# The bias stage of an attention and two-layer kernel: where two splits run, and on which engine four masks are made

## The chip, the cores and the metric

The kernel runs on one core of a Trainium2 chip. The metric is the device time of one execution in microseconds (us). The core has five engines with a queue each: TensorE (PE, matmuls into PSUM), VectorE (DVE), ScalarE (ACT), GpSimd (POOL) and SyncE (SP), which here only issues DMAs. PEld is PE's weight load, which is shown apart.

## The reference

Three steps follow one another; all is fp32.

- Attention over 4 batches, 8 heads, 576 positions, head size 64: `scores = q @ k.T / 8 + bias`, a softmax, and the product with `v`. The bias is the same for every batch. It comes from a small network of the relative position: `x[i,j] = log1p(|i-j|) / log1p(max(i,1))`, `h = relu(x * w1 + b1)` with 32 hidden units, `bias = h @ w2`, one value for each head.
- A dense layer with a leaky activation: 2304 tokens, 512 to 2048 and back to 512.
- A soft routing: 32 slots get a softmax-weighted mean of the tokens, each of 8 experts runs two layers on its 4 slots, and each token gets a softmax-weighted mean of the slots' results.

## The kernel before

The program runs through the bias stage (about the first 75 us), attention for 16 pairs (a pair of heads and a batch each, about 13 us a pair), the dense layer with the routing beside it, and the experts. It is written in a framework that plans the order of each engine's queue offline, by simulated times and by the order in which the instructions stand in the program. `keep_in_program_order(ins)` (a pin) ties an instruction behind the instruction of the same engine that stands before it in the program; without a pin the plan may move it.

**Bias stage** (`bias_phase`, lines 70 to 285). A relu of a linear function of x is a linear function where x is above a threshold and zero elsewhere. So the stage makes masks (is log1p(|i-j|) above the threshold of this hidden unit?), and matmuls sum them, weighted, into two accumulators a0 and a1; the bias is `a0 * x + a1`. The work goes in nine rounds k = 0 to 8 over relative distance. A round has 16 masks of 576 columns or, from round 5 on, 512, 384, 256 and 128 (`make_mask`, line 135), in a ring of 40 (`RING`): mask u of round k reuses the place of the mask that was made 40 earlier. Table `ENGS` says by a letter which engine makes each mask: A is ACT with a steep sigmoid (line 142), V is DVE with a comparison (line 144). A round has up to five units c = 3, 2, 1, 0 and, in rounds 0 to 4, 4 (`unit`, line 148). A unit is 48 matmuls (16 masks by 3 parts of the weights, line 160) into one of four accumulators, then its evacuation on DVE: a product (line 189) and a sum into `rows` (line 193, or 191 for c = 4). Then POOL writes the mirrored half of `rows` (line 211; called a flip here). When a chunk of rounds is complete, SP stores the rows into W in DRAM (line 216). The masks of round k + 1 are written between the units of round k (lines 264 to 275).

`att.load(0)` and `att.load_v(0)` load pair 0 before the rounds, `att.load(1)` and `att.load_v(1)` stand behind them. `att.bias_first(s)` (line 347) loads the bias of the first pair of heads back from W, piece s, at the end of rounds 5 and 7 and behind the rounds. The stores for the other heads (`late`) come last.

**Attention** (`Attention`, line 288). Each of q and k of a pair is split into a high half, rounded to the matmul format, and a low half, the rest (`split`, line 371): k = 0 makes `qh` (1216 columns), 1 `ql`, 2 `kh` (576 columns), 3 `kl`, all on POOL (lines 380 and 382). For pair 0 the four stand at the ends of rounds 0 to 3 of the bias stage:

```python
if k < 4:
    att.split(0, k)
```

For pair 1 they stand at the head of `run` (line 545), and none of the eight is pinned. In the trace POOL runs both pairs' splits between 14 and 30 us. Later pairs are split two pairs ahead. `raw`, the loaded pair, has two buffers. Scores are matmuls of line 412, 60 for a pair; then DVE adds the bias and takes the minimum (`z`, line 435), ACT takes the exponential (line 455), PE transposes (line 475), ACT or DVE copies (lines 491 and 489), and PE multiplies with v (line 503). Attention's order is written out by hand in `ROUND`, and from pair 1 on all of it is pinned.

Of the kernel before, what the change touches and what calls it, by code (L numbers as in the profile page):

```python
# [8 lines left out]
F32 = mybir.dt.float32  # L9
# [4 lines left out]
AF = mybir.ActivationFunctionType  # L14
ALU = mybir.AluOpType
# [26 lines left out]
TAGS = ("cfgc", "becb", "gbd", "ada", "mnm")  # L42
LATE, EARLY = "bcdg", "aefmn"
ENGS = (
    "VVVAVVAVVAVVAVVA", "AAAVAAAVAAAVAAAV", "AAAVAAAVAAAVAAAV", "AAAVAAAVAAAVAAAV", "AAAVAAAVAAAVAAAV", "AAVAAVAAVAAVAAVA",
    "AAVAAVAAVAAVAAVA", "AVAAVAVAAVAVAAVA", "AVAVAVAAVAVAVAVA",
)
LA = 5
# [18 lines left out]
BIG = float(2.0 ** 20)  # L67


def bias_phase(tc, ident, W, W4, cpack, lcol, prow, xmain, xtail, att):  # L70


    nc = tc.nc
    with ExitStack() as ctx:
# [13 lines left out]
        pr = cp.tile([P, S], F16, name="pr")  # L88
# [10 lines left out]
        wb = cp.tile([P, NTQ], F32, name="wb")  # L99
# [27 lines left out]
        for k in range(3):  # L127
            eng = nc.gpsimd if k < 2 else nc.vector
# [6 lines left out]
        def make_mask(k, u):  # L135

            t = 16 * k + u
            n = min(S, 128 * (NG - k))
            dst = mask[:, t % RING, :n]
            on = ENGS[k][u]  # L140
            if on == "A":
                nc.scalar.activation(dst, pr[:, :n], AF.Sigmoid, bias=wb[:, t : t + 1], scale=BIG)  # L142
            else:
                nc.vector.tensor_scalar(dst, pr[:, :n], wl[:, t : t + 1], None, ALU.is_gt)

# [2 lines left out]
        def unit(k, c):  # L148
# [4 lines left out]
            if c < 4:  # L153
                m, cols, dst = P, slice(P * c, P * c + P), acc
            else:
                m, cols = 64 * (k % 2) + 64, slice(512, S)
                dst = acc[m - 64 : m]
# [12 lines left out]
            i = max(n for n in range(len(ks)) if ks[n] <= k)  # L170
# [14 lines left out]
            fwd = both[:m, :, :, w + f0 : w + f0 + 64]  # L185
            tmp = cp.tile([P, H, 2, 32], F32, tag="tmp", name=f"tmp{k}_{c}", bufs=2)
            xb = xs.rearrange("p (s j) -> p s j", s=2).unsqueeze(1).to_broadcast([m, H, 2, 32])
            a0, a1 = (acc[:m, :, n].rearrange("p s h j -> p h s j") for n in range(2))
            nc.vector.tensor_tensor(tmp[:m], a0, xb, ALU.mult)
            if c == 4:  # L190
                nc.vector.tensor_tensor(fwd[:, :, 0].rearrange("p h (s j) -> p h s j", s=2), tmp[:m], a1, ALU.add)
            else:
                nc.vector.tensor_tensor(  # L193
                    fwd.rearrange("p a b (s j) -> p a b s j", s=2),
                    tmp[:m].rearrange("p (a b) s j -> p a b s j", b=2),
                    a1.rearrange("p (a b) s j -> p a b s j", b=2),
                    ALU.add,
                )

            one = d0 == 0 and c < 4  # L200
            z = int(one and f0 == 0)
            a = both[:m, :, :, w + one - f0 - 64 : w + one - f0 - z]
            if c == 4:
                a, src = a[:, :, 0], fwd[:, :, 0]
            else:
                src = fwd[:, :, :, z:]
            e = a.ap[-1][0]
            back = bass.AP(
                tensor=a.tensor, offset=a.offset + (63 - z) * e, ap=[list(v) for v in a.ap[:-1]] + [[-e, 64 - z]]
            )  # L210
            nc.gpsimd.tensor_scalar(back, src, 1.0, 1.0, ALU.mult, ALU.mult)
            if not last:
                return

# [42 lines left out]
        for u in range(16):  # L257
            make_mask(0, u)
# [5 lines left out]
        for k in range(NG):  # L264
            cs = [c for c in range(3, -1, -1) if k <= NG - 1 - c]
            if k < 5:
                cs.append(4)
            done = 0
            for n_, c in enumerate(cs):
                unit(k, c)  # L270
                if k + 1 < NG:
                    upto = 16 * (n_ + 1) // len(cs)
                    for u in range(done, upto):
                        make_mask(k + 1, u)
                    done = upto
            if k < 4:
                att.split(0, k)
            if k in (5, 7):
                att.bias_first(k // 7)
        att.load(1)  # L280
# [7 lines left out]
class Attention:  # L288
# [82 lines left out]
    def split(self, i, k):  # L371

        st = self.st[i]
        x = "qk"[k // 2]
        src = st["raw"][:, :1216] if x == "q" else st["raw"][:, 1216:]
        if k % 2 == 0:
            st[x, 0], st[x, 1] = (
                self.sp.tile([P, src.shape[1]], F32R, tag=x + "hl"[n], name=f"{x}{'hl'[n]}{i}") for n in range(2)
            )
            self.nc.gpsimd.tensor_scalar(st[x, 0], src, 1.0, 1.0, ALU.mult, ALU.mult)  # L380
        else:
            self.nc.gpsimd.tensor_tensor(st[x, 1], src, st[x, 0].bitcast(F32), ALU.subtract)  # L382

    def late(self, i, ins):

# [865 lines left out]
def kernel(  # L1251
# [17 lines left out]
        for n, b in (("a_raw", 2), ("a_v", 3), ("a_split", 2))  # L1269
    )  # L1270
    bias_phase(tc, ident, W, W4, cpack, lcol, prow, xmain, xtail, att)

    kp = ctx.enter_context(tc.tile_pool(name="m_keep", bufs=1, reuse_waits="tile"))
# [178 lines left out]
```

## Time and profile before

| | us |
|---|---|
| median of 3 runs | 804.72 (804.67 to 805.17) |
| the profiled execution | 801.72 |
| its span, first to last instruction | 799.9 |

| engine | busy us | share of the span | instructions |
|---|---|---|---|
| PE | 760.0 | 95% | 7438 |
| DVE | 531.0 | 66% | 999 |
| ACT | 503.5 | 63% | 1053 |
| POOL | 323.8 | 40% | 283 |

A row of instructions has the start in us, the time in us, engine, line, operation, output<-inputs, shapes and count; in brackets the idle time of the engine before it and what ended that. "issue" means that the engine waited for nothing that the profile shows. Times of single instructions overlap a little from one to the next.

### The profile page before, as it was taken

To read this page: it belongs to the slowest core of one execution; us is meant where nothing else is said; L and a number is where in the kernel's file an instruction comes from. 1 tells how busy PE (TensorE), PEld (TensorE's weight loads), DVE (VectorE), ACT (ScalarE), POOL (GpSimd) and SP (SyncE) were. 2 spreads that over 40 slices of the span, in tenths; PEclk is the share of its full clock that TensorE was granted. 3 is DMA by queue.
4 is the path that set the end of the run, shared out by engine and by line. 5 is a ranking of instruction groups with operands and counts; after the bars stand their busy time and mean duration, and the time that the engine had idled before them with its cause. 6 is when DMAs were issued, how large, how long until landed. Compare 5 with 4: busy or idle time off the path is not lost.

```text
span 799.9 us, 18597 instructions
## 1 busy us (share of the span) xinstructions
PE 760.0 (95%) x7438; PEld 636.4 (80%) x7438; DVE 531.0 (66%) x999; ACT 503.5 (63%) x1053; POOL 323.8 (40%) x283
## 2 busy tenths in 40 slices
PE   6877899999999999999999999999999999999994
PEld 6876777777787778999898888888889898887431
DVE  8878788888898856776777566546654746544203
ACT  8973788888888854444456666656665656654102
POOL 4723253646465713114225554445553551240000
PEclk9999799999999999999999999999999999999898
DMA  6597975738444641433420011301100124349895
GB/s 202 141 251 198 307 242 199 237 95 297 145 123 152 186 159 63 141 119 105 147 90 1 1 40 41 131 1 41 40 1 21 40 78 159 107 134 358 318 376 237
DMA packets 48406, 114.44 MB, mean 143 GB/s; under 512 B 10433, under 2 KB 29761, under 8 KB 46273
## 3 DMA queue, kind: packets, MB, share of 16 engines
q1 hardware_dynamic: 48320, 113.26, 43.0%
q8 instruction: 58, 0.95, 0.5%
q14 instruction: 28, 0.22, 0.1%
HBM read 91.95 MB, written 21.29 MB: 142 GB/s over the span
## 4 chain that ended last, share of the span: by engine, by line
PE 80%; DVE 4%; DMA 4%; ACT 1%; issue 1%; POOL 1%; SPq 0%; DVEq 0%; ACTq 0%
PE ys L757 25%; PE h L728 24%; PE o L503 9%; PE s L412 8%; PE t L475 4%; PE ops L1211 3%; PE hps L1211 2%; DVE z L435 1%; DMA W<-rows 1%; PE acc L160 1%; PE lp L826 1%; DMA raw<-in_qk_dram 1%; DMA em<-in_mw_dram 1%; DMA nb<-W 1%; DMA rs<-rt 1%
## 5 line engine op out<-in xcount | busy, mean ns | idle before, releaser
L739 DVE SCALAR_TENSOR_TENSOR g<-g,nal 128x384 f32<-128x384 f32 x96 | 70.2, 731 | 93.8 <-ACT g L738 93.8
L435 DVE CUSTOM_DVE_ANT_0 z<-s,nb 128x576 f32<-128x576 f32 x144 | 108.0, 754 | 18.0 <-PE s L412 9.4
L455 ACT ACTIVATE e<-z,m 128x576 f32<-128x576 f32 x144 | 109.9, 767 | 7.6 <-DVE m L435 7.6
L736 ACT ACTIVATE g<-h 128x384 f32<-128x384 f32 x96 | 47.1, 490 | 64.8 <-PE h L728 63.5
L491 ACT ACTIVATE g<-t 128x640 f32<-128x640 f32 x96 | 67.3, 703 | 30.7 <-PE t L475 26.6
L503 PE MATMUL o<-g,v 128*64 128x256 f32 (+1 forms) x640 | 85.3, 411 | 0.5 <-ACT g L491 0.5
L744 DVE TENSOR_TENSOR gr<-g,gr 128x384 fp32r<-128x384 f32 x80 | 63.7, 797 | 29.2 <-ACT gr L742 29.1
L475 PE MATMUL t<-ident,e 64*128 64x64 f32 x1440 | 69.1, 225 | 5.4 <-DVE m L435 4.3
L475 PEld LDWEIGHTS t<-ident,e 64*128 64x128 f32 x1440 | 66.5, 141 | 7.4 <-issue 5.5
L160 PE MATMUL acc<-wp,mask 128*128 128x64 bf16 (+1 forms) x1680 | 57.2, 199 | 15.7 <-issue 6.6
L742 ACT ACTIVATE gr<-g 128x384 fp32r<-128x384 f32 x96 | 50.3, 524 | 34.3 <-DVE g L739 34.1
L160 PEld LDWEIGHTS <-mask 128*128 128x128 bf16 (+1 forms) x1680 | 55.5, 104 | 17.3 <-DVE rows L193 6.4
L503 PEld LDWEIGHTS o<-g,v 128*64 128x64 f32 x640 | 43.3, 136 | 28.4 <-ACT g L491 1.0
L412 PE MATMUL s<-kh,qh 64*128 64x288 f32 x320 | 62.1, 384 | 1.3 <-DVE rows L193 0.7
L142 ACT ACTIVATE mask<-pr,wb 128x576 bf16<-128x576 f16 (+4 forms) x94 | 54.8, 675 | 8.1 <-PE acc L160 8.0
L412 PE MATMUL s<-kh,ql 64*128 64x288 f32 x320 | 48.5, 298 | 0.0
L412 PE MATMUL s<-kl,qh 64*128 64x288 f32 x320 | 48.5, 298 | 0.0
L744 POOL TENSOR_TENSOR gr<-g,gr 128x384 fp32r<-128x384 f32 x16 | 19.2, 1200 | 71.9 <-ACT gr L742 51.9
L738 ACT ACTIVATE g<-h 128x384 f32<-128x384 f32 x96 | 46.7, 487 | 0.0
L380 POOL TENSOR_SCALAR qh<-raw 128x1216 fp32r<-128x1216 f32 x16 | 19.5, 1218 | 66.7 <-PE s L412 61.3
L382 POOL TENSOR_TENSOR ql<-raw,qh 128x1216 fp32r<-128x1216 f32 x16 | 44.9, 2807 | 0.0
L412 PEld LDWEIGHTS s<-kh,qh 64*128 64x128 f32 x320 | 31.5, 192 | 10.5 <-DVE r L522 4.2
(851 smaller groups left out, 1838.8 us busy)
## 6 DMA issues: line engine op xcount, KB each, us to landing
wide<-in_w_dram SPq DMA_DIRECT2D x16, 1024.0 KB
ep<-in_mw_dram SPq DMA_DIRECT2D x29, 512.0 KB
raw<-in_qk_dram SPq DMA_DIRECT2D x16, 896.0 KB
nb<-W SPq DMA_DIRECT2D x3, 2304.0 KB
v<-in_v_l_dram SPq DMA_DIRECT2D x16, 320.0 KB
pre<-in_mw_dram SPq DMA_DIRECT2D x10, 512.0 KB
ex<-in_mw_dram SPq DMA_DIRECT2D x9, 512.0 KB
W<-rows SPq DMA_DIRECT2D x14, 256.0 KB
```

Of the source, the lines that this page charges most:

```text
L142: nc.scalar.activation(dst, pr[:, :n], AF.Sigmoid, bias=wb[:, t : t + 1], scale=BIG)
L160: nc.tensor.matmul(dst[:, u // 8, :, :, 4 * (u % 8) : 4 * (u % 8) + 4], mask[:, (16 * k + u) % RING, cols], wp[:, part], start=part == 0, ...
L412: nc.tensor.matmul(s[:, hf, :288], st["q", a][d, o : o + P], st["k", b][d, 288 * h : 288 * h + 288], start=n_ == 0, stop=n_ == len(seq) - 1,),
L435: self.nc.vector.tensor_tensor_reduce(out=z.rearrange("p (a b) -> p a b", a=2), in0=s[:, :, :288], in1=nb.rearrange("p (a b) -> p a b", a= ...
L455: self.nc.scalar.activation(e, z, AF.Exp, bias=m, scale=-1.0, accum_out=st["sum"][:, slot : slot + 1]),
L475: self.pin(i, nc.tensor.transpose(tp[:, r, 64 * c : 64 * c + 64], e[q, k0 : k0 + P], self.ident[q, q]))
L491: self.pin(i, nc.scalar.activation(dst, src, AF.Copy))
L503: nc.tensor.matmul(op[64 * h : 64 * h + 64, 0, :n], st["v"][:, h, c], g[:, h, c], start=c == 0, stop=c == 4),
L728: nc.tensor.matmul(h, w_[:, c * P : (c + 1) * P], x_[:, c], start=c == 0 and n_ == 0, stop=c == NC - 1 and n_ == 2,)
L739: nc.vector.scalar_tensor_tensor(g, neg, self.nal[:, f : f + 1], g, ALU.mult, ALU.add)
L744: eng.tensor_tensor(gl, g, gh.bitcast(F32), ALU.subtract)
L757: i = self.nc.tensor.matmul(self.ys[blk][t], g_[:, t * P : (t + 1) * P], w_, start=f == 0 and n_ == 0, stop=f == NF - 1 and n_ == 2,)
```

## The change

In the bias stage:

- `ENGS`: rounds 1 to 4 have 11 masks on ACT and 5 on DVE, where they had 12 and 4.
- Pair 0's split leaves the ends of rounds 0 to 3. Its high halves `qh` and `kh` are copies on ACT, behind round 5's masks (end of round 4); its low halves `ql` and `kl` are subtractions on DVE, at the end of round 5. All four are pinned.
- Pair 1's split stays on POOL and is pinned, so that it stands behind all flips.
- Masks on ACT, the sums into `rows` on DVE and the flips on POOL are pinned.

```diff
-    "VVVAVVAVVAVVAVVA", "AAAVAAAVAAAVAAAV", "AAAVAAAVAAAVAAAV", "AAAVAAAVAAAVAAAV", "AAAVAAAVAAAVAAAV", "AAVAAVAAVAAVAAVA",
+    "VVVAVVAVVAVVAVVA", "AAVAAVAAVAAVAAVA", "AAVAAVAAVAAVAAVA", "AAVAAVAAVAAVAAVA", "AAVAAVAAVAAVAAVA", "AAVAAVAAVAAVAAVA",
...
-                nc.scalar.activation(dst, pr[:, :n], AF.Sigmoid, bias=wb[:, t : t + 1], scale=BIG)
+                i = nc.scalar.activation(dst, pr[:, :n], AF.Sigmoid, bias=wb[:, t : t + 1], scale=BIG)
+                tc.keep_in_program_order(i)
...
+            tc.keep_in_program_order(i_)
...
-            nc.gpsimd.tensor_scalar(back, src, 1.0, 1.0, ALU.mult, ALU.mult)
+            tc.keep_in_program_order(nc.gpsimd.tensor_scalar(back, src, 1.0, 1.0, ALU.mult, ALU.mult))
...
-            if k < 4:
-                att.split(0, k)
+            if k in (4, 5):
+                att.split(0, k - 4)
+                att.split(0, k - 2)
...
-            self.nc.gpsimd.tensor_scalar(st[x, 0], src, 1.0, 1.0, ALU.mult, ALU.mult)
+            if i == 0:
+                self.early(1, self.nc.scalar.activation(st[x, 0], src, AF.Copy))
+                return
+            self.early(i, self.nc.gpsimd.tensor_scalar(st[x, 0], src, 1.0, 1.0, ALU.mult, ALU.mult))
         else:
-            self.nc.gpsimd.tensor_tensor(st[x, 1], src, st[x, 0].bitcast(F32), ALU.subtract)
+            eng = self.nc.gpsimd if i else self.nc.vector
+            self.early(max(i, 1), eng.tensor_tensor(st[x, 1], src, st[x, 0].bitcast(F32), ALU.subtract))
+
+    def early(self, i, ins):
+
+        if i == 1:
+            self.tc.keep_in_program_order(ins)
```

## Rows read from the trace of the kernel before

**Rows 1.** The page, part 1: busy us, share of the span, instructions.

```profile
PE 760.0 (95%) x7438; PEld 636.4 (80%) x7438; DVE 531.0 (66%) x999; ACT 503.5 (63%) x1053; POOL 323.8 (40%) x283
```

**Rows 2.** Windows: length, each engine's busy us, granted clock, DMA share, GB/s.

```profile
13.80:31.00 17.20, 13.18 (x376) 12.82 (x374) 17.09 (x20) 17.20 (x27) 16.58 (x15) 0.90 0.29 109
51.90:74.90 23.00, 19.66 (x620) 19.12 (x616) 22.94 (x47) 9.59 (x24) 9.26 (x14) 1.00 0.79 180
80.00:90.00 10.00, 8.21 (x88) 7.27 (x88) 7.25 (x19) 6.93 (x16) 0.00 (x0) 0.57 1.01 281
100.00:110.00 10.00, 10.00 (x147) 7.68 (x144) 8.33 (x21) 8.13 (x19) 7.50 (x6) 1.00 1.02 364
```

**Rows 3.** Waits of PE, 0 to 75 us: total us, times, longest us.

```profile
PE acc L160 <- issue: 6.6, 5, 2.6
...
PE acc L160 <- DVE rows L193: 3.5, 2, 2.2
```

**Rows 4.** Timeline of PE around 30 us.

```profile
30.52 9.81 PE L160 MATMUL acc<-wp,mask 128*128 128x64 bf16 x298 [2.20 <-DVE rows L193]
```

**Rows 5.** Timeline of DVE in the bias stage.

```profile
16.84 4.35 DVE L144 TENSOR_SCALAR mask<-pr,wl 128x576 bf16<-128x576 f16 x2
...
30.99 0.42 DVE L144 TENSOR_SCALAR mask<-pr,wl 128x576 bf16<-128x576 f16 x1
...
36.14 0.36 DVE L144 TENSOR_SCALAR mask<-pr,wl 128x576 bf16<-128x576 f16 x1
...
51.93 1.29 DVE L189 TENSOR_TENSOR tmp<-acc,xm_t 128x512 f32<-128x512 f32 x2 [3.69 <-PE acc L160]
```

**Rows 6.** Groups of DVE, 13.8 to 31 us: count, busy us, mean ns, idle before.

```profile
L144 DVE TENSOR_SCALAR mask<-pr,wl 128x576 bf16<-128x576 f16 x8 | 10.9, 1401 | 0.0
```

**Rows 7.** Timeline of POOL in the bias stage.

```profile
16.80 2.78 POOL L382 TENSOR_TENSOR ql<-raw,qh 128x1216 fp32r<-128x1216 f32 x1
...
74.92 0.68 POOL L211 TENSOR_SCALAR rows<-rows 128x512 f32<-128x512 f32 x1 [0.62 <-DVE rows L193]
```

**Rows 8.** Timeline of ACT in the bias stage.

```profile
5.23 45.19 ACT L142 ACTIVATE mask<-pr,wb 128x576 bf16<-128x576 f16 x70
52.92 4.64 ACT L142 ACTIVATE mask<-pr,wb 128x384 bf16<-128x384 f16 x10 [2.50 <-PE acc L160]
61.62 3.57 ACT L142 ACTIVATE mask<-pr,wb 128x256 bf16<-128x256 f16 x10 [4.07 <-PE acc L160]
```

**Rows 9.** Windows of line 160 alone: PE, PEld, clock, DMA share, GB/s.

```profile
25.69:35.49 9.80, 7.59 (x243) 7.30 (x240) 1.00 0.54 155
35.49:44.29 8.80, 7.97 (x243) 7.57 (x241) 1.00 1.07 308
44.29:51.69 7.40, 4.79 (x123) 4.70 (x120) 0.77 1.09 326
```

**Rows 10.** Window of pair 2's split: POOL is the fifth busy time.

```profile
95.40:101.60 6.20, 6.20 (x102) 4.98 (x96) 5.19 (x12) 5.50 (x12) 6.01 (x4) 1.00 0.99 409
```

**Rows 11.** Window of line 412 alone, up to pair 1's first scores.

```profile
73.60:87.76 14.16, 7.19 (x60) 5.63 (x62) 0.77 0.84 251
```

**Rows 12.** Groups over the whole span: busy us, mean ns, idle before.

```profile
L491 ACT ACTIVATE g<-t 128x640 f32<-128x640 f32 x96 | 67.3, 703 | 30.7 <-PE t L475 26.6
...
L682 DVE SCALAR_TENSOR_TENSOR wr<-wide,wr 128x1024 uint32<-128x1024 uint32 x14 | 17.1, 1222 | 0.3
...
L716 DVE TENSOR_TENSOR w47o<-wr,w47o 128x512 fp32r<-128x512 f32 x1 | 0.7, 693 | 0.9 <-ACT w47o L715 0.9
```

**Rows 13.** The chain of waits at the end of the stage: start us, us, what.

```profile
70.60 0.67 POOL rows L211
...
71.59 4.42 DMA W<-rows
...
77.04 3.72 DMA W<-rows
...
80.83 4.98 DMA nb<-W
```

More of the change, by code (lines that the diff above doesn't have):

```diff
@@ L190, in unit @@
             if c == 4:
-                nc.vector.tensor_tensor(fwd[:, :, 0].rearrange("p h (s j) -> p h s j", s=2), tmp[:m], a1, ALU.add)
+                i_ = nc.vector.tensor_tensor(fwd[:, :, 0].rearrange("p h (s j) -> p h s j", s=2), tmp[:m], a1, ALU.add)
             else:
-                nc.vector.tensor_tensor(
+                i_ = nc.vector.tensor_tensor(
                     fwd.rearrange("p a b (s j) -> p a b s j", s=2),
```

## The prediction

> **What bounds the kernel now.** I read the page first: TensorE (PE) is busy 95% of the span of 799.9 us [rows 1]. An average over stages says little about a change in the first 75 us, so the table of windows came next. From 13.8 to 31 us PE is busy 13.18 of 17.20 us and VectorE (DVE) 17.09; from 51.9 to 74.9 PE 19.66 of 23.00 and DVE 22.94 [rows 2]. So PE has room in the bias stage, and DVE is full at its beginning and at its end. From 100 us on PE is busy 10.00 of 10.00 us [rows 2]: attention is paced by PE, so what the stage gains or loses arrives at the end of the kernel one for one. The question is only how much earlier the stage hands over.
>
> The waits of the stage [rows 3]: PE stopped five times, 6.6 us in all, up to "issue": it waited for no semaphore that the profile shows, and none of the edits names a cause of that. It stopped twice, 3.5 us, for DVE's `rows`: an accumulator was not free, because DVE was late in emptying it. The larger of the two, 2.20 us, ends at 30.52 [rows 4].
>
> DVE's rows say why it was late then. From 13.8 to 31 us it made eight masks in 10.9 us, 1401 ns each [rows 6]; an undisturbed mask of that shape is the one at 36.14 us, 0.36 us [rows 5]. Beside them GpSimd (POOL) ran the splits of pairs 0 and 1: the two masks that start on DVE at 16.84 take 4.35 us [rows 5], while `ql` on POOL runs from 16.80 for 2.78 us [rows 7] and `kl` after it. So the eight masks took 10.9 - 8 x 0.36 = 8.0 us of DVE more than they take alone.
>
> ScalarE (ACT) makes 70 masks without a gap from 5.23 us on, 45.19 us, so 0.645 us each, and then waits for PE, 2.50 us and later 4.07 [rows 8]. At 50.4 us it is ahead of PE, not behind: on the chip its masks no longer hold PE in rounds 3 and 4. That matters for the third edit below.
>
> **Part by part.** All sums are made against the profiled execution (span 799.9, execution 801.72 us). The median of the three timed runs, 804.72, lies 3.0 us above it; the difference found is applied to that.
>
> *Pair 0's split leaves POOL's early rounds, pair 1's goes behind the stage.* DVE's 8.0 us go. Only what PE waited for can reach the end, and that is its one stop on DVE there: -2.2 us [rows 4]. The rest of the 8.0 becomes idle time of DVE, since rounds 1 to 3 are then fed as fast as PE runs. Late next is PE itself: round 2 keeps it busy 7.59 us in a window of 9.80 [rows 9].
>
> *Pair 1's split, now behind the last flip.* That flip starts at 74.92 and takes 0.68 us [rows 7]. A pair's four split operations take POOL 6.01 us [rows 10], so they are done at 81.6. PE needs them for the first scores of pair 1; pair 0's 60 matmuls of line 412 fill the window up to 87.76, and pair 1 follows [rows 11]. The cover is 6 us, and both ends move with the stage: cost 0. Nothing else is queued on POOL before pair 2's split, and no DMA is added; the load of pair 3, which needs the buffer that this split frees, is issued a round of attention later. On the gaining side, the flips of rounds 0 to 3 no longer queue behind a `ql` of 2.8 us, so SyncE's first W stores may leave up to that much earlier, into a stretch in which the DMA engines are 0.29 busy [rows 2]; I take 0 for it.
>
> *Pair 0's high halves on ACT, behind the masks of round 5.* Scaled by columns from the 640-column copy of 703 ns [rows 12]: 0.703 x (1216 + 576)/640 = 2.0 us. Scaled by the masks' 0.645 us for 576 columns it would also be 2.0. Behind them wait round 6's masks. ACT idles 2.50 us in that round and 4.07 in the next, for PE [rows 8], so cost 0; without that cover, round 6 would start up to 2.0 us late.
>
> *One mask of each of rounds 1 to 4 from ACT to DVE.* ACT -4 x 0.645 = -2.6 us; DVE +4 x 0.36 = +1.4, or 4 x (0.36 + 0.68) = 4.2 if each waits for a flip on POOL. Another mask beside POOL's work, at 30.99, took 0.42 [rows 5], so nearer the first. DVE has them where it has just lost 8.0 us of delay: cost 0. On ACT the gain is worth nothing directly, since ACT is ahead of PE. It can matter for the written order: in round 4, from 44.29 on, PE loads 120 masks before DVE starts the next evacuation at 51.93 [rows 5, 9], where one unit is 48, because PE's order interleaves a round's units around masks that were planned to come late. With ACT's masks planned earlier there is less to interleave. Ends: 0, and all of the 72 matmuls beyond one unit, 72 x 7.59/243 = 2.2 us [rows 9]. No row says which; I take -1.3, a little over the middle, because by round 4 the plan too has been relieved of 2.6 us of ACT.
>
> *Pair 0's low halves on DVE in round 5.* Operations with two inputs from SBUF: 693 ns at 512 columns, 1222 at 1024 [rows 12], so 1.03 ns a column: 1.42 us for 1216 columns and 0.76 for 576, together 2.2. They stand behind a mask of round 6 whose place in the ring comes free in round 4's last unit, so they fall in the stretch from 51.9, where DVE is busy 22.94 of 23.00 us [rows 2]. Behind them wait the evacuations of rounds 5 to 7, and for those POOL's flips and the last W stores. Ends: 0, if they find gaps or stand behind the last evacuation, and 2.2. The nearest row is that of a full DVE, so most of it counts; but where round 4's first evacuation comes earlier, gaps open between units, since PE takes 1.5 us for a unit (48 x 7.59/243) and DVE 1.3 (two operations of 0.65, [rows 5]): +1.5.
>
> On this edit the page "SBUF — State Buffer" of the Trainium skill, section "Summary: rules for kernel authors", speaks against the change: an operation of VectorE with two SBUF inputs fully blocks against a GpSimd operation that reads SBUF, as one in a 2-port fast mode does. The flips read SBUF and run through that whole stretch. The trace shows such a block for masks only (4.35 us for two). By the rule `ql` and `kl` would wait for a flip each, at most 2 x 0.68 us, and the sum would be 1.4 us higher; without it, it stays.
>
> *The hand-over.* The chain of waits runs from a flip at 70.60 through a W store (4.42 us), the issue of a bias load, a second store (3.72) and the last bias load (4.98) to `z` [rows 13]. It begins with an evacuation of round 7, so it moves with DVE.
>
> Sum: -2.2 - 1.3 + 1.5 = -2.0 us. Profiled, 801.72 becomes 799.7; the median 804.72 becomes **802.7 us**.
>
> **Rivals.** *Given back on DVE.* PE's order stays as it is, round 4's first evacuation comes 2.2 us earlier, at 49.7, and the whole 2.2 of `ql` and `kl` stands in the gapless stretch: 804.7. For it: 22.94 of 23.00 us. Against: the counts of masks change, so the plan changes.
>
> *The gaps cover it.* All 2.2 us of interleaving go, and `ql` and `kl` fall into gaps: -2.2 - 2.2 = -4.4, so 800.3. For it: PE then paces the stage's end. Against: 0.2 us of DVE a unit is little for masks and 2.2 us more.
>
> *Slower: the low halves decide.* PE's stops up to "issue" fall where they will; one of 2.60 us lies in round 4, in a window where the DMA engines are 1.09 busy [rows 9]. If what PE gains at 30 us is lost in such a stop, round 4's first evacuation still begins at 51.9, and the full stretch behind it grows by 2.2: 804.72 + 2.2 = 806.9, or 808.3 if each of the two also waits for a flip of 0.68. It decides from the point where that first evacuation begins at 51.9 or later.
>
> *The transfers keep their own pace.* The stage is over 2 us earlier, but stores and bias loads take the time back: the DMA engines are 1.01 busy from 80 to 90 us [rows 2]. 804.7. Against: the chain waits for a flip first, and from 51.9 to 74.9 the engines are 0.79 busy [rows 2].
>
> That the change doesn't do what it says would mean masks that stay slow beside the flips alone. A flip is 0.68 us, not 2.8, and most masks of the full stretch were not slow; no chance of its own.
>
> **Numbers.** Forecast 0.45 (its own range 801.4 to 804.0), gaps 0.16, given back 0.16, transfers 0.08, slower 0.15. A measurement of this kernel can tell about 0.2%, 1.6 us, from no change, so faster is under 803.1. Of the forecast's share 0.32 lies under that, 0.13 within. Faster 0.32 + 0.16 = 0.48; same 0.13 + 0.16 + 0.08 = 0.37; slower 0.15. The range leaves out the far ends of the two outer cases: 799.8 to 806.0.
>
> **What would show it.** Right: masks on DVE at 0.36 to 1.0 us from 14 to 31 us; no stop of PE on `rows` near 30; round 2 over by 33.5; the first evacuation of round 4 between 47 and 50; `ql` and `kl` on DVE at 1.4 and 0.75 us; pair 1's split done before pair 1's first scores; the last bias load landing near 84. Wrong: that first evacuation at 51.9, a PE stop ahead of pair 1's scores, or a stage that ends earlier while `z` still waits until 86 for its bias.

## The result and the profile after

Timed side by side, the kernel before took 804.72 us (median of 5 executions, 803.34 to 806.02) and the changed one 798.76 us (5 executions, 796.42 to 799.45): ratio 0.9917, 95% interval 0.9898 to 0.9937. By the medians that is -6.0 us, where the sum said -2.0; three of the five executions of before are those that the prediction started from. The forecast, 802.7 us, had the sign right and lay 3.9 us too high, and 798.76 is under its range, 799.8 to 806.0. The same two kernels were compared three times more, on three different chips (the chip of the first comparison is not on record):

| comparison | before, us (executions) | changed, us (executions) | ratio, 95% interval |
|---|---|---|---|
| first | 804.72 (5) | 798.76 (5) | 0.9917, 0.9898 to 0.9937 |
| second | 799.55 (35) | 797.61 (12) | 0.9974, 0.9957 to 0.9990 |
| third | 800.79 (35) | 797.09 (12) | 0.9963, 0.9940 to 0.9987 |
| fourth | 800.11 (20) | 795.99 (12) | 0.9957, 0.9940 to 0.9975 |

By the ratios the last three give -2.1, -3.0 and -3.4 us (by the medians of the table -1.9, -3.7 and -4.1). Between the first profiled executions of the two kernels the difference is 801.72 - 798.79 = 2.9 us; 801.72 is not one of the five timed ones. The changed kernel's 798.79 is at its own median; the kernel before was timed 3.0 us above its profile in the first comparison only.

Part 1 of the page after [rows 1]:

```profile
PE 759.5 (95%) x7438; PEld 635.5 (80%) x7438; DVE 526.5 (66%) x1005; ACT 502.3 (63%) x1051; POOL 317.4 (40%) x279
```

Windows of the changed kernel that answer to [rows 2]: the same early window, and the one from round 4's first evacuation to DVE's last `rows`.

```profile
13.80:31.00 17.20, 14.78 (x439) 14.45 (x436) 13.67 (x27) 17.20 (x27) 5.42 (x8) 0.90 0.56 210
45.32:70.25 24.93, 21.01 (x656) 20.28 (x653) 24.20 (x49) 14.03 (x32) 9.67 (x14) 1.00 0.75 172
```

Waits of PE from 0 to 75 us [rows 3]; the matmuls' line is 161 now, that of `rows` 194:

```profile
PE acc L161 <- issue: 3.6, 3, 2.3
PE acc L161 <- DVE rows L194: 2.0, 3, 1.2
```

The group of DVE's masks from 13.8 to 31 us [rows 6]:

```profile
L145 DVE TENSOR_SCALAR mask<-pr,wl 128x576 bf16<-128x576 f16 x10 | 3.7, 408 | 0.9 <-PE acc L161 0.8
```

From 13.8 to 31 us PE does 439 matmuls in place of 376, DVE is busy 13.67 us, not 17.09, and a mask takes 408 ns in place of 1401. Windows of the matmuls' line alone for rounds 2, 3 and 4 [rows 9]:

```profile
26.03:33.61 7.58, 7.46 (x242) 7.30 (x240) 1.00 0.98 308
33.61:41.69 8.08, 7.69 (x244) 7.36 (x240) 1.00 1.03 290
41.69:50.35 8.66, 7.66 (x244) 7.38 (x240) 1.00 1.07 219
```

Round 2 takes 7.58 us, not 9.80, of which PE works 7.46: nothing but PE paces it. Timeline of DVE [rows 5]:

```profile
45.32 1.29 DVE L190 TENSOR_TENSOR tmp<-acc,xm_t 128x512 f32<-128x512 f32 x2 [1.61 <-PE acc L161]
...
53.83 1.42 DVE L389 TENSOR_TENSOR ql<-raw,qh 128x1216 fp32r<-128x1216 f32 x1
...
55.76 0.74 DVE L389 TENSOR_TENSOR kl<-raw,kh 128x576 fp32r<-128x576 f32 x1
...
69.56 0.69 DVE L194 TENSOR_TENSOR rows<-tmp,acc 128x512 f32<-128x512 f32 x1
```

The last line is the end of the stage on DVE; in the kernel before it was

```profile
74.14 0.69 DVE L193 TENSOR_TENSOR rows<-tmp,acc 128x512 f32<-128x512 f32 x1
```

Timeline of ACT [rows 8]:

```profile
45.17 1.20 ACT L384 ACTIVATE qh<-raw 128x1216 fp32r<-128x1216 f32 x1
46.28 0.67 ACT L384 ACTIVATE kh<-raw 128x576 fp32r<-128x576 f32 x1
...
56.26 3.56 ACT L142 ACTIVATE mask<-pr,wb 128x256 bf16<-128x256 f16 x10 [1.75 <-PE acc L161]
```

Timeline of POOL [rows 7, 10]:

```profile
55.92 1.06 POOL L213 TENSOR_SCALAR rows<-rows 64x512 f32<-64x512 f32 x1 [3.21 <-DVE rows L192]
...
70.97 1.22 POOL L386 TENSOR_SCALAR qh<-raw 128x1216 fp32r<-128x1216 f32 x1
...
75.74 1.43 POOL L389 TENSOR_TENSOR kl<-raw,kh 128x576 fp32r<-128x576 f32 x1
```

Round 4's first evacuation starts at 45.32, not 51.93; the stage ends on DVE at 70.25, not 74.83. ACT copies the high halves (no table load stands before them in the trace) and waits for PE afterwards (1.75 us). Pair 1's split is done at 77.2. The window of the scores' line alone [rows 11] shows pair 0's 60 matmuls filling the time up to 83.0:

```profile
69.00:83.00 14.00, 7.20 (x60) 5.63 (x62) 0.70 0.79 244
```

The chain of waits at the stage's end [rows 13] still runs through two W stores, and the last bias load is issued at 75.90 (the line of SPq, SyncE's queue), which was 80.83. The last `z` that waits for a bias load starts at 77.97, which was 85.97:

```profile
72.14 3.70 DMA W<-rows
...
75.90 0.33 SPq L346
...
76.28 3.99 DMA W<-rows
```

Not all of the 4.6 us on DVE arrives in this pair of executions. Behind the stage PE runs at granted clock 0.50 (the lower of its two levels, 1.2 GHz) from 74.5 to 84.7 us and in this execution again from 88.1 to 91.5; in the kernel before there was one such stretch there, from 81.4 to 91.6. Window of that second stretch in the changed kernel:

```profile
88.10:91.50 3.40, 3.40 (x24) 1.95 (x22) 0.20 (x2) 2.21 (x5) 0.00 (x0) 0.50 0.82 288
```

PE is busy in all of it, so it loses half of the 3.4 us, some 1.7. Pair 1's scores start 4.8 us earlier than before (83.0 against 87.8), pair 2's 2.5 (100.4 against 102.9), and the span is 2.9 us shorter (797.0). Over all profiles of the two kernels (three of before, four of the changed one) the spans are 798.7 and 795.2 us in the mean, 3.4 apart.

### The profile page after: what moved, and what is told of

Same layout as the page of the kernel before. It is cut to its first block, busy times and chain, and to the rows that moved or that the text cites. A ratio compares the mean times of both kernels' runs of the same rounds, so it can differ in the third digit from the quotient of the medians.

```text
span 797.0 us, 18598 instructions
## 1 busy us (share of the span) xinstructions
PE 759.5 (95%) x7438; PEld 635.5 (80%) x7438; DVE 526.5 (66%) x1005; ACT 502.3 (63%) x1051; POOL 317.4 (40%) x279
## 4 chain that ended last, share of the span: by engine, by line
PE 81%; DVE 4%; DMA 3%; ACT 1%; issue 1%; SPq 1%; POOL 0%; DVEq 0%; ACTq 0%; POOLq 0%
PE h L740 24%; PE ys L769 24%; PE o L515 10%; PE s L424 8%; PE t L487 5%; PE ops L1223 3%; PE hps L1223 2%; DMA ex<-in_mw_dram 1%; DVE z L447 1%; DMA W<-rows 1%; PE lp L838 1%; PE sp L1021 1%; DVE r L533 1%; DMA rs<-rt 0%; PE sp L889 0%
## 5 line engine op out<-in xcount | busy, mean ns | idle before, releaser
L751 DVE SCALAR_TENSOR_TENSOR g<-g,nal 128x384 f32<-128x384 f32 x96 | 70.2, 732 | 93.3 <-ACT g L750 93.3
L161 PEld LDWEIGHTS <-mask 128*128 128x128 bf16 (+1 forms) x1680 | 53.9, 103 | 13.6 <-DVE mask L145 5.4
L142 ACT ACTIVATE mask<-pr,wb 128x576 bf16<-128x576 f16 (+4 forms) x90 | 52.0, 667 | 3.9 <-PE acc L161 3.8
L389 POOL TENSOR_TENSOR ql<-raw,qh 128x1216 fp32r<-128x1216 f32 x15 | 42.0, 2803 | 0.1
```

Source lines behind the costliest of these rows:

```text
L142: i = nc.scalar.activation(dst, pr[:, :n], AF.Sigmoid, bias=wb[:, t : t + 1], scale=BIG)
L161: nc.tensor.matmul(dst[:, u // 8, :, :, 4 * (u % 8) : 4 * (u % 8) + 4], mask[:, (16 * k + u) % RING, cols], wp[:, part], start=part == 0, ...
L751: nc.vector.scalar_tensor_tensor(g, neg, self.nal[:, f : f + 1], g, ALU.mult, ALU.add)
```

## Experiments

Theory: the trace of before accounts for the change (stop on `rows` gone, less interleaving, longer full stretch of DVE). Rivals: one of the edits does nothing or harm, or what differs between the executions is not in the edits at all. From the second comparison on, the question was the size.

**The kernel before, again (no edit).**

> The kernel before once more, unchanged. Every theory expects a ratio of 1.00. It gives a second profiled execution: before was timed at 803.3 to 806.0 us but profiled at 801.7, while after was profiled at its own median. If the first profile was a lucky one, the span here is near 803 us and the stage's stops of PE up to 'issue' are longer than 6.6 us, or PE runs longer at its lower clock between 80 and 95 us. If the profile was typical, the span is again 799.9 and the missing 3 us lie outside the span.

800.12 us against 800.34 in the same comparison, 1.0003 (0.9987 to 1.0019). The 35 executions of the kernel before beside it lay between 797.44 and 804.66: one execution of the same program can be 7 us longer than another. The profiled one is shorter than the first (span 798.0, not 799.9), and PE stands idle up to "issue" for 2.4 us before 75 us, where [rows 3] has 6.6. Neither of the two outcomes named above came, and the first profile was not a lucky one.

**Pair 1's split alone behind the stage.** Pair 0's split stays on POOL in rounds 0 to 3; the masks' counts are the old ones; the three pins are kept. Against the kernel before only POOL's order differs in the traces; the lines, against the kernel before:

```
+            self.early(i, self.nc.gpsimd.tensor_scalar(st[x, 0], src, 1.0, 1.0, ALU.mult, ALU.mult))
...
+            self.early(i, self.nc.gpsimd.tensor_tensor(st[x, 1], src, st[x, 0].bitcast(F32), ALU.subtract))
```

> Only pair 1's split goes behind the stage; pair 0's stays on POOL in rounds 0 to 3. The written orders of PE, DVE and ACT are those of before, instruction for instruction. Theory A (DVE's delay beside POOL is the cost, and PE's one stop on rows pays it): the masks at 25.7 to 29.8 us take 0.3 to 0.8 us each, the stop of 2.2 us at 30 us is gone or under 0.5, round 4's first evacuation begins 2 us earlier and the time falls by 2 to 3 us, with no price on DVE at the end. Theory B (the order, changed by the mask counts, brings the gain): within 0.5 us of before.

798.49 us, 0.9976 (0.9957 to 0.9996), so -1.9 us for this edit alone, with an interval from -3.4 to -0.3. Group of DVE's masks from 13.8 to 31 us:

```profile
L145 DVE TENSOR_SCALAR mask<-pr,wl 128x576 bf16<-128x576 f16 x8 | 7.3, 949 | 0.3 <-PE acc L161 0.3
```

PE's waits from 0 to 75 us:

```profile
PE acc L161 <- issue: 5.5, 4, 2.9
...
PE acc L161 <- DVE rows L194: 3.0, 6, 1.3
```

With pair 1's part of POOL's work gone from there a mask takes 949 ns, and the stop of 2.2 us near 30 us is gone: the longest wait for `rows` is 1.3 us. Theory A's earlier first evacuation of round 4 can't be read from this one trace: it begins at 48.48, 3.4 us ahead of the first profile of before but level with its second and third (48.28 and 48.84), because PE stood idle up to "issue" for 5.5 us ahead of it, and for 1.7 and 1.8 us there.

**Both splits moved, masks as before** (lines against the changed kernel; the pins stay).

```
-    "VVVAVVAVVAVVAVVA", "AAVAAVAAVAAVAAVA", ... (rounds 1 to 4)
+    "VVVAVVAVVAVVAVVA", "AAAVAAAVAAAVAAAV", ...
```

> Both splits moved as in the change, mask counts as before (12 and 4). Theory A: most of the gain, -3 to -6 us; round 4's first evacuation still comes after some 120 matmuls of the round. Theory B: -0.3 us or none, since 2.2 us gained at 30 us are paid back by the two low halves on DVE.

799.47 us, 0.9991 (0.9971 to 1.0012): theory A's -3 to -6 us is out. **Masks alone** (the other way round: the kernel before with the new ENGS, and so without the pins):

> Only the four masks move from ACT to DVE; the splits stay on POOL in rounds 0 to 3. Theory A: no gain or a loss of up to 2 us, since DVE gets four more masks where POOL delays it. Theory B: -2 us, because PE's written order interleaves the units of rounds 2 to 4 less and round 4's first evacuation begins 2 us earlier.

800.27 us, 0.9997 (0.9979 to 1.0015): theory B's -2 us is out. Windows of the matmuls' line from the start of round 4 to its first evacuation, in the kernel before (second profile), with the splits alone, with the masks alone, and in the changed kernel; the count behind the second busy time is that of weight loads:

```profile
43.60:48.28 4.68, 3.96 (x130) 3.73 (x127) 1.00 1.01 365
```
```profile
41.70:46.31 4.61, 4.00 (x131) 3.76 (x128) 1.00 0.87 281
```
```profile
44.30:49.92 5.62, 4.45 (x150) 4.33 (x147) 1.00 1.04 351
```
```profile
41.69:45.32 3.63, 2.74 (x91) 2.61 (x88) 1.00 1.04 285
```

The interleaving falls only in the whole change: 127 loads, 128, 147, and then 88. The masks alone lack the three pins as well as the moved splits, so which of the two the new masks need is not shown; the pins and the splits without the new masks leave PE's order as it was before. With the splits alone the stop near 30 us is gone too, but from round 4's first evacuation to the last `rows` it takes 25.1 us, where before took 22.9; the masks alone make the interleaving worse and leave two stops of PE for `rows` near 30 us.

**The changed kernel, again (no edit).**

> The changed kernel once more, unchanged, on the chip where before takes 800.3 us. Theory C (the kernel gains what the stage's hand-over gains, about 2 to 4 us, and the rest of the first 6 us lay in the first five runs of before, which were 803 to 806 us): 796.5 to 798.5 us, ratio 0.995 to 0.998. Theory D (the change is worth 0.8% anywhere): 793.5 to 794.5 us, ratio 0.992.

797.61 us, 0.9974 (0.9957 to 0.9990): -2.1 us, the size of the forecast, and its interval does not meet that of the first comparison.

**Low halves behind the stage** (against the changed kernel).

```
-            if k in (4, 5):
-                att.split(0, k - 4)
-                att.split(0, k - 2)
+            if k == 4:
+                att.split(0, 0)
+                att.split(0, 2)
+            if k == 8:
+                att.split(0, 1)
+                att.split(0, 3)
```

> The change with pair 0's two low halves on DVE at the end of round 8 instead of round 5; the copies on ACT stay. Theory A (the 2.2 us of low halves stand in a full DVE and are paid once): the evacuations end 1.5 to 2.2 us earlier after round 4's first evacuation than in after, that stretch is 23 us and not 24.9; the time falls by up to 2 us against after if pair 0's first scores can wait, and not at all if the hand-over through W's stores does not move. The rival (gaps cover the low halves): no difference from after.

797.07 us, 0.9973 (0.9955 to 0.9990), 0.5 us under the changed kernel beside it. The full stretch is 23.4 us, as theory A has it, and the last `rows` ends at 67.0, but `ql` and `kl` now stand between it and the first `z`, which starts at 70.2 (70.8 in the changed kernel of the same comparison): the two operations can be put off, not saved.

**Low halves behind round 3** (high halves behind round 2):

> The change with pair 0's high halves on ACT at the end of round 2 and its low halves on DVE at the end of round 3, where DVE has gaps in after. Theory A: the stretch from round 4's first evacuation to the last one shrinks by 2 us, round 4 begins no later, and the time is 1.5 to 2 us under after. The rival (DVE or ACT paces PE in rounds 2 to 4 as well): round 4 begins 1 to 2 us later and the time is that of after.

796.41 us, 0.9956 (0.9936 to 0.9977); and in the third comparison

> The version with pair 0's high halves on ACT behind round 2 and its low halves on DVE behind round 3, a second time on other executions. If the low halves belong where DVE has just been freed of the delays of POOL, it stays 0.5 to 2 us under the changed kernel (0.995 to 0.997 of the kernel before). Rival: the 1.2 us of the last comparison were scatter, and it lies within 0.4 us of the changed kernel on either side.

796.95 us, 0.9954 (0.9933 to 0.9974), 0.1 us under the changed kernel there, where it had been 1.2 us under it before. **Halves behind rounds 3 and 4:**

> Only the place of pair 0's split differs from the changed kernel: high halves on ACT behind round 3, low halves on DVE behind round 4. PE's order has round 4's last unit spread over 80 matmuls, as in the changed kernel, where the version a round earlier has 93; DVE gets the low halves ahead of the evacuations of round 5 rather than of round 6. If the interleaving decides (1.2 us for some 40 matmuls), it beats the version a round earlier by up to 0.4 us. If the full stretch of DVE decides (1.5 to 2.0 us for the low halves), it comes out near the changed kernel, 1 us above the version a round earlier, with a tail from round 4's first evacuation to the last rows near 24.9 us instead of 22.9.

797.84 us, 0.9975 (0.9954 to 0.9996). Windows of all engines (DVE third) from round 4's first evacuation to the last `rows`: first with the halves behind rounds 3 and 4, then with the low halves behind round 3 (second profile).

```profile
47.69:72.72 25.03, 21.03 (x657) 20.28 (x653) 25.00 (x49) 11.37 (x28) 9.51 (x15) 1.00 0.64 168
```
```profile
45.85:69.01 23.16, 20.52 (x640) 19.80 (x637) 22.68 (x48) 13.19 (x32) 10.04 (x16) 1.00 0.81 200
```

`ql` in the timeline of DVE, in the same order:

```profile
48.30 1.42 DVE L392 TENSOR_TENSOR ql<-raw,qh 128x1216 fp32r<-128x1216 f32 x1
```
```profile
34.62 1.42 DVE L392 TENSOR_TENSOR ql<-raw,qh 128x1216 fp32r<-128x1216 f32 x1
```

At 34.6 us the low halves fall into time that DVE has to spare; at 48.3 they lengthen the full stretch, 25.03 us against 23.16. So their place decides what they cost on DVE, 1.9 us; of that only 0.1 to 1.2 us shows in the times.

**Pair 1's loads behind round 1's stores** (changed kernel, `att.load(1)` and `att.load_v(1)` moved to `k == 1` and kept in program order):

> The change with pair 1's two loads issued behind the stores of round 1 instead of before all stores; the written orders of the four compute engines are those of after, instruction for instruction. If PE's first stop up to 'issue' (at 16 us, 1.2 to 3.1 us long in every profile so far) comes from transfers that fill the DMA engines between 8 and 16 us, it shrinks under 0.5 us, round 1 begins at 15.5 and not at 17, and the time falls by 1 us or more unless ACT's masks of round 1 (ready at 16.5) hold it. If the stop has nothing to do with them, it stays at 1.2 us or more.

799.64 us, 0.9996 (0.9977 to 1.0014): 2 us slower than the changed kernel beside it. PE's stop ahead of matmul 223, 1.71 us beside it, is 0.15; that ahead of matmul 862, 1.93 us beside it, is 3.85. A stop that a transfer can take away and another can lengthen has a cause in the DMA engines. The trace has it: among the packets are 58 of a queue called instruction, on the page of before

```profile
q8 instruction: 58, 0.95, 0.5%
```

that is 0.95 MB / 58 = 16.4 KB each, and PE's 2 x 7438 instructions [rows 1] over 58 are 256: 128 matmuls with their weight loads. PE's stops up to "issue" lie at matmuls 223, 351, 606, 734, 862, 989, ..., one or two such blocks apart. Timeline of PE in the kernel before:

```profile
41.17 4.14 PE L160 MATMUL acc<-wp,mask 128*128 128x64 bf16 x127 [0.83 <-issue]
47.91 1.28 PE L160 MATMUL acc<-wp,mask 128*128 128x64 bf16 x21 [2.60 <-issue]
```

The DMA queues of the same kernel (packets, MB, share of 16 engines), first from 41.20 to 45.40 us, then from 45.40 to 45.60, where a packet counts in the window in which it starts:

```profile
q1 hardware_dynamic: 1239, 1.48, 109.2%
...
q1 hardware_dynamic: 24, 0.07, 95.4%
q8 instruction: 1, 0.02, 34.0%
```

From 41.2 to 45.4 the DMA engines carry data alone, with 1239 packets; the next instruction packet starts only at 45.5, when PE has used up its 127 matmuls, and lands at 46.6; PE goes on at 47.9. In the 17 traces of this study PE stops so over 80 times by over 0.2 us in the bias stage, and each time it goes on 1.2 to 2.0 us after such a packet has landed (all but two of them 1.2 to 1.7). In the first three profiles of each of the two kernels, the packet starts 0.2 to 1.6 us into the block of matmuls ahead of it where the DMA engines were under a quarter busy, and PE stops by 0.3 us at most; where they were over 0.7 busy, it starts 0.9 to 4.3 us into the block. (Such a stop is taken from the start of one matmul to the start of the next, and left out where PE also waited for a semaphore; the place of a packet is counted from the first matmul of the block.)

**The changed kernel a third time, and the kernel before a third profile (no edits).**

> The changed kernel, unaltered, a third time, to settle which of the two sizes is its own: -6.0 us (0.9917, first comparison) or -2.1 us (0.9974, second). Theory A: the change is worth what the traces account for, 2.0 to 2.5 us (PE's stop on rows, 38 matmuls less ahead of round 4's evacuation, less the longer tail), and the first comparison caught the kernel before in its slower executions: ratio 0.9965 to 0.9985, the kernel before again at 799 to 801. Theory B: the change also shortens stretches that no profile of mine caught, and the second comparison was the exception: ratio 0.991 to 0.994, the kernel before again at 804 or more.

797.09 us, 0.9963 (0.9940 to 0.9987): -3.0 us, between the two theories' bands and nearer to the first.

> The kernel before, unaltered, once more on the chip of these runs, for another profile. If PE's stops up to issue and its half-clock stretches belong to the execution and not to the program's order, they fall at the same matmul numbers as in the other two profiles of it, with another sum: between 3.4 and 7.6 us in the first 75 us. If they belong to the order, the sum repeats within 0.5 us.

800.08 us, 0.9996 (0.9968 to 1.0023). PE's stops up to "issue" sum to 4.74 us from start to start of the matmuls around them, ahead of matmuls 223, 989, 1117, 1500 and 1628, which are all starts of blocks; the other two profiles of the kernel before have 7.60 and 3.39. Their sum belongs to the execution. So do the half-clock stretches inside the stage: they start at 16.5 and 47.2 us in the first profile, at 16.0 in the second and at 30.8 in the third.

**The changed kernel a fourth time.**

> The changed kernel, unaltered, a fourth time. Three comparisons gave -6.0, -2.1 and -3.0 us. Theory: the edits themselves are worth 2 to 3 us, and the rest of the first comparison was PE's stops up to issue, which end 1.2 to 1.6 us after a 16 KB packet of PE's instructions has landed and grow when that packet stands behind data in the DMA engines; their sum in the first 75 us was 3.4 to 7.6 us in three profiles of the kernel before and 4.8 to 6.5 in three of the changed one, so it favours neither. Expected: ratio 0.995 to 0.999, and in the profile every stop of PE up to issue ends 1.2 to 1.7 us after such a packet. Rival: the change is worth 5 us or more and the second and third comparisons were the exceptions: ratio under 0.994.

795.99 us, 0.9957 (0.9940 to 0.9975), -3.4 us, inside the theory's band; its four stops of this kind (5.04 us) all end 1.3 to 1.6 us after an instruction packet has landed.

**Pair 1's loads behind round 3's, or round 5's, stores** (on the version with the low halves behind round 3; moved as above, to `k == 3` or `k == 5`):

> The version with the low halves behind round 3, and pair 1's loads of 896 and 320 KB issued behind round 3's W stores (near 45 us) instead of at 8 us. If PE's stops are its instruction packets standing behind data, the stop ahead of matmul 223, 1.2 to 3.1 us in every profile with the early loads, falls under 0.4 us, its packet starting near 12 us instead of 13.0 to 14.5, and stops grow at the packets that now stand beside those loads (matmuls 989 to 1245, 44 to 55 us). If the stops belong to PE's order or to a fixed place of the program, the one ahead of matmul 223 stays at 1.2 us or more. Time: within 1.5 us of the same version with early loads, since the loads' bytes only change which packet they delay.

796.63 us, 0.9949 (0.9934 to 0.9963). Timeline of PE, first with the early loads, then with the late ones:

```profile
11.81 2.25 PE L161 MATMUL acc<-wp,mask 128*128 128x64 bf16 x65
16.24 1.94 PE L161 MATMUL acc<-wp,mask 128*64 128x64 bf16 x56 [2.17 <-issue]
```
```profile
11.83 6.34 PE L161 MATMUL acc<-wp,mask 128*128 128x64 bf16 x200
```

Window from 10 to 14 us in the same order; the DMA share is the last but one number:

```profile
10.00:14.00 4.00, 4.00 (x133) 3.94 (x130) 3.90 (x7) 4.00 (x7) 1.35 (x2) 1.00 1.03 408
```
```profile
10.00:14.00 4.00, 4.00 (x126) 3.95 (x123) 3.90 (x7) 4.00 (x7) 1.36 (x2) 1.00 0.49 183
```

And the DMA queues with the late loads, from 12.20 to 12.40 us:

```profile
q8 instruction: 1, 0.02, 30.5%
q1 hardware_dynamic: 5, 0.01, 18.3%
```

With 1.2 MB less in the DMA engines the packet starts at 12.3, not 13.9, and PE runs through. All 14 traces with early loads have that stop, 1.19 to 3.11 us; the three with late loads 0.03, 0.15 and 0.28. The expected growth did not come where I put it: the loads were issued at 51.0, matmuls 989 to 1245 kept their packets, and the one ahead of matmul 1500 started 3.5 us into its block and cost 2.60 us. The version with early loads was not timed on this chip; the changed kernel, 795.99 there, is the nearest.

> The same with pair 1's loads behind round 5's W stores (near 57 us). The stop ahead of matmul 223 under 0.4 us again, and those in rounds 2 to 4 (matmuls 606 to 1117) no longer than in the version with early loads, 3 to 5 us together. The loads then lie where DVE and not PE paces the stage, so stops of PE there cost less: 1 to 2 us faster than with early loads. Rival: pair 1's split on POOL, which needs the load at 68 to 70 us, comes late, and PE waits for it ahead of pair 1's scores: 1 us or more slower, with a stop of PE on POOL near 80 us.

797.48 us, 0.9957 (0.9942 to 0.9973). The stop ahead of matmul 223 is 0.28, those of rounds 2 to 4 make 3.8 us, and yet nothing is gained; nor is pair 1's split late (done at 74.1, scores at 82.2). The first `z` waits 1.68 us for its bias load, which now is issued behind pair 1's loads: a third outcome that neither theory had. No version here beats the changed kernel by more than the comparisons' uncertainty.

## Why the prediction was wrong in size

**The step that failed is the base.** The prediction said: "The median of the three timed runs, 804.72, lies 3.0 us above it; the difference found is applied to that." It took those 3.0 us for a property of the kernel, which the changed one would keep. They did not come back, so they were no property of the kernel. The kernel before has medians of 799.6 to 800.8 in the four later comparisons, and the profiled executions of its two copies took 799.77 and 799.85; the changed kernel's profile and median agree (798.79 and 798.76). Of the 3.9 us by which 802.7 was too high, 3.0 are this. Made against the profiled execution alone the same sum said 799.7, 0.9 above what came. That this is so near is in part luck: 798.76 is itself 1.2 to 2.8 us above the changed kernel's later medians.

**PE's stops were held constant.** "None of the edits names a cause of that" was true of the edits, but the page of before held the queue that names it. In that first profile the stops ahead of matmuls 862 and 989 make 3.82 us; in the other two 0.00 and 1.01. With the second of them, which left PE idle from 45.3 to 47.9, the clock fell: from 47.2 to 50.6 us PE ran at 1.2 GHz, which neither of the others does there.

```profile
47.20:50.60 3.40, 2.69 (x51) 2.68 (x51) 1.04 (x2) 3.22 (x7) 1.25 (x2) 0.50 1.12 320
```

Its 51 matmuls took 2.69 us, 53 ns each, where [rows 9] has 7.59 / 243 = 31 ns at full clock: 1.1 us more. Stops and clock together are why round 4's first evacuation stands at 51.93 in the first profile, and at 48.28 and 48.84 in the others. The prediction had that window's clock, 0.77, before it [rows 9] and made nothing of it. Whether long stops or a lower clock also made the timed executions of the first comparison slow isn't shown, since those have no trace; it stays open. The bound of 0.2% for a measurement was too small for five executions: on one chip 35 of the kernel before spread from 797.44 to 804.66. In part this spread goes with the granted clock: of the 145 later executions of the kernel before, the 36 with a mean clock of 0.984 or more took 799.4 us in the mean, the 18 with 0.978 or less 802.1. But the spread alone does not make the first comparison: only 10 of the 145 took 803.34 us or more, and there all five did. So five draws from that spread are an unlikely explanation; a condition common to those five, such as their chip, is another, and no run tells them apart.

**The terms**, over three profiles of before and four of after:

- Stop on `rows`, -2.2: right. It is in all three of before (2.2 us near 30) and in none of after, and pair 1's split alone gave -1.9 us (-3.4 to -0.3). That one pair's split off POOL is enough was not foreseen.
- Interleaving, -1.3: right in size, 40 loads fewer x 7.59 / 243 [rows 9] = 1.2 us. The reason was not the whole of it: the new masks alone, without the moved splits and the pins, made it worse (147 loads).
- Low halves, +1.5: right. `ql` and `kl` take 1.42 and 0.74 us, and the full stretch is 24.94, 24.94, 24.24 and 24.33 us against 22.91, 22.95 and 23.36: +1.5 in the mean. The rival in which gaps cover them falls.
- ACT copies, pair 1's split, hand-over, each 0: right by the rows above. The first evacuation at 45.3 was outside the 47 to 50 that I named, and the flip beside `kl`, not `kl`, was the one to wait: it started 0.16 us later and took 1.06 us, where the same flip took 0.61 in the kernel before; on POOL that costs nothing. With the low halves behind the stage `kl` had to wait for a flip, and took 1.19 us.
- Together: the stage's end on DVE goes from 72.8 to 70.0 in the mean, -2.7 us, where the sum said -2.0 and the last three comparisons -2.1 to -3.4. The rest of 0.7 is round 4's first evacuation, 4.3 us earlier and not 3.5; with stops of 3.4 to 7.6 us in these profiles I can't say which edit owns it.

So the rivals "given back on DVE", "the transfers keep their own pace" and "slower" are out, by all four comparisons.

## What to carry to other kernels

A sum made from one traced execution forecasts a difference from that execution; when timed runs lie elsewhere than the trace, ask for the reason before adding the offset, and repeat the comparison on other executions before explaining a size. Work on POOL beside masks on DVE cost PE a stop of 2.2 us here, and moving half of that work ended it. Where an engine stops for nothing the semaphores show, look in the DMA queues for its own instructions.

## What the runs showed of the hardware

PE's instructions come in 16 KB packets through the same DMA engines as the data. A packet behind full queues started up to 5.3 us into the block of 128 matmuls ahead of it, which lasts about 4 us at full clock, and PE went on 1.2 to 2.0 us after it had landed; these stops make 3.4 to 8.0 us of the first 75, with no semaphore in the trace. The Trainium skill, page "Runtime: NRT & Kernel Launch", section "Instruction fetch mechanics", says that instructions are refilled in blocks of 16 KiB (256 instructions) through the sequencer's own DMA queue, and that the cost is mostly hidden. The size agrees with these traces (58 packets for 14876 instructions); that it is hidden holds here only where the DMA engines have room: under a quarter busy, PE stopped by 0.3 us at most.
